# Attention, gated MLP and routed experts on one core: second rows ahead of weights, later conversions, sink work moved to other engines and queues, three fillers

## Chip, cores and metric

The kernel runs on 1 core of one Trainium2 chip. The metric is the device time of one launch in microseconds (us), inputs and outputs in HBM; lower is better.

## What is computed

Three layers, one after the other, all in float32 from outside:

```
scores = q @ k.T / sqrt(64)            # 2 batches, 8 heads, 768 tokens, head size 64
keep   = (key < 4) | (0 <= query - key < 128)      # 4 sink columns and a window
x = softmax(where(keep, scores, -1e9)) @ v         # heads side by side: 1536 x 512
x = (silu(x @ w_gate) * (x @ w_val)) @ w_out       # 512 -> 1536 -> 512
skip = x @ w_skip > 0                              # rows that are computed
e, g = argmax, softmax probability of x @ w_gate2  # one of 8 experts
out  = x + g * (relu(x @ w1[e]) @ w2[e])           # else out = x
```

The three weights of the middle layer come as 64-bit numbers and are turned into float32 on the chip.

## The kernel before

**Staging.** The 1536 tokens are 12 blocks of 128 (block n; six blocks to a batch), in three groups of four. The attention of the first group runs alone; this stretch is called the prologue here. Then the first phase of the MLP starts: TensorE works through the gate, value and down projections of the first group, and the attention of the next blocks and the conversion of the later weights are played between its matmuls from a written score (`beside_first_phase`, `first_phase`). Two more MLP phases, the routing and the experts follow.

**One block of attention.** A block has four head pairs; step j is pair `pr` of block `n`, j = 4n + pr. `step_a` turns k and q of a pair on TensorE (`tqk`, L315) and copies them from PSUM to the tile `kq` (L320); for the first block of a batch GpSimd copies the four sink columns (L331). `step_b` makes the scores (`s`, L363), merges two key blocks by a predicated copy (L369), adds the mask and takes the maximum on VectorE (L380), and takes the exponential on ScalarE (L385), two instructions for a pair. Then it copies the four sink columns of the two heads to `psk` (L399). `step_d` turns the probabilities (`tpt`, L412), copies them out (`pt`) and cuts them by two selections on GpSimd (L422, L423). `step_s` splits the sink columns of a block into a high and a low part (`ps`, L430 and the helper L81) and turns them (`tsk`, L434); `step_e` adds all products with the values (`xps`, L452, L469), divides by the sums (`rps`, L460, L476) and writes the turned block `xt`, high and low, which the MLP reads. `load_sinks` (L277) brings the values of the sink tokens to the tile `vst` and spreads them to `vs` (L291).

**Weights.** `load_w` loads one chunk of 128 columns (or rows) of a weight, 512 KB as 64-bit numbers, to one of three staging buffers `st` (L160). `convert` makes float32 of it: two ScalarE instructions (L175, L176), then two VectorE instructions (L181, L182); then the next chunk is loaded. Chunks come as gate, value, out. `filler` puts matmuls on an idle tile at a very low priority, to be placed where TensorE would wait (L619), `warm` nineteen of them at the start (L608).

**What sets the order.** In the prologue the framework's scheduler orders the instructions of each engine by priorities that follow the order in the code, under the dependencies; each engine then executes its list strictly in order, and a wait of its first instruction holds all that are behind it. An `issue_after` ties an instruction behind another. The first four conversions are tied behind instructions that are noted in `begun`. DMAs of SyncE (SP) and ScalarE are issued in the order of those lists. The loop that drives it all (from L1507) advances attention by one piece per turn (a "pull"), adds fillers, and converts a weight whenever `converted < 12 * pulls // 56`. From the first phase on the order is written by hand and is the same in both kernels, apart from a few fillers at its start.

## Time and profile before

| what | value |
|---|---|
| median of 3 runs | 599.38 us (597.09 to 600.08) |
| profiled execution, its own time | 596.77 us |
| its span (first to last instruction) | 594.4 us |
| TensorE busy | 562.4 us (95%) |
| VectorE, ScalarE, GpSimd busy | 447.1 (75%), 355.1 (60%), 216.5 us (36%) |
| first matmul of the MLP starts at | 63.67 us |
| mean granted TensorE clock | 0.987 |

Times in the rows below count from the start of the span. The profiled execution's own time is 2.37 us longer than its span (launch and end), and lies 2.6 us below the median of the runs. A busy share is an average over stages with different limits, and a TensorE that is shown busy may be waiting inside a pipelined matmul. In a row of the timeline the number behind the start is the duration, and the bracket says how long the engine had been idle and who released it.

### The profile page before, as it was taken

To read this page: it belongs to the slowest core of one execution; us is meant where nothing else is said; L and a number is where in the kernel's file an instruction comes from. 1 tells how busy PE (TensorE), PEld (TensorE's weight loads), DVE (VectorE), ACT (ScalarE), POOL (GpSimd) and SP (SyncE) were. 2 spreads that over 40 slices of the span, in tenths; PEclk is the share of its full clock that TensorE was granted. 3 is DMA by queue.
4 is the path that set the end of the run, shared out by engine and by line. 5 is a ranking of instruction groups with operands and counts; after the bars stand their busy time and mean duration, and the time that the engine had idled before them with its cause. 6 is when DMAs were issued, how large, how long until landed. Compare 5 with 4: busy or idle time off the path is not lost. (4 is left out here: it accounts for less than half of the span.)

```text
span 594.4 us, 10013 instructions
## 1 busy us (share of the span) xinstructions
PE 562.4 (95%) x3052; PEld 437.3 (74%) x3052; DVE 447.1 (75%) x1104; ACT 355.1 (60%) x854; POOL 216.5 (36%) x325
## 2 busy tenths in 40 slices
PE   7999899998999999999999999999998899889992
PEld 4666677786778777787778888888885687667872
DVE  4898587878887899965555999775375797989930
ACT  4798687876776665555454453545164775856710
POOL 3354274676486242413320100040144334525301
PEclk8799999999999999999999999999999999999998
DMA  8896254695523413000004432320268876868501
GB/s 202 196 247 168 83 161 141 178 291 150 162 33 97 139 28 81 1 19 1 18 9 145 149 103 66 99 81 21 84 218 245 276 254 218 313 219 295 187 4 38
DMA packets 90341, 80.53 MB, mean 135 GB/s; under 512 B 53515, under 2 KB 65803, under 8 KB 90274
## 3 DMA queue, kind: packets, MB, share of 16 engines
q1 hardware_dynamic: 87138, 73.01, 41.4%
q0 software_dynamic: 2848, 6.74, 3.7%
q8 instruction: 29, 0.48, 0.3%
q14 instruction: 38, 0.31, 0.2%
q10 hardware_dynamic: 288, 0.00, 0.0%
HBM read 70.09 MB, written 12.00 MB: 138 GB/s over the span
## 5 line engine op out<-in xcount | busy, mean ns | idle before, releaser
L660 PE MATMUL gv<-xt,ring 128*128 128x512 f32 x864 | 218.1, 400 | 1.7 <-ACT xt L78 1.5
L660 PEld LDWEIGHTS gv<-xt,ring 128*128 128x128 f32 x864 | 158.3, 188 | 40.7 <-issue 2.5
L78 ACT ACTIVATE ring<-w 128x512 fp32r<-128x512 f32 x113 | 70.8, 628 | 71.1 <-PE gv L660 54.8
L81 DVE TENSOR_TENSOR w<-stage,w 128x512 fp32r<-128x512 f32 x99 | 87.6, 924 | 4.8 <-ACT w L78 3.4
L78 ACT ACTIVATE w<-stage 128x512 fp32r<-128x512 f32 x128 | 74.2, 627 | 19.8 <-DMA stage<-in_moe_w_dram 15.6
L673 PE MATMUL acc<-ring,hh 128*128 128x512 f32 x256 | 82.4, 403 | 0.0
L81 DVE TENSOR_TENSOR ring<-w,ring 128x512 fp32r<-128x512 f32 x77 | 53.8, 699 | 25.3 <-ACT ring L78 21.6
L81 POOL TENSOR_TENSOR w<-stage,w 128x512 fp32r<-128x512 f32 x29 | 39.9, 1380 | 88.5 <-DVE ring L81 60.1
L81 POOL TENSOR_TENSOR ring<-w,ring 128x512 fp32r<-128x512 f32 x36 | 48.8, 1362 | 32.1 <-ACT ring L78 30.3
L673 PEld LDWEIGHTS acc<-ring,hh 128*128 128x128 f32 x256 | 46.3, 188 | 11.7 <-issue 1.0
L869 DVE CUSTOM_DVE_ANT_0 wl<-x,wl 128x512 f32<-128x512 f32 x72 | 51.5, 716 | 1.3
L673 PE MATMUL acc<-ring,hl 128*128 128x512 f32 x128 | 50.6, 396 | 0.0
L1226 PE MATMUL yps<-w,hT 128*128 128x512 f32 x192 | 48.3, 401 | 0.8 <-ACTq L1265 0.4
L422 POOL TENSOR_SCALAR_AFFINE_SELECT pt<-pt 128x256 f32<-128x256 f32 x40 | 23.6, 591 | 67.7 <-ACT pt L78 67.7
L385 ACT ACTIVATE p<-p,st 128x132 f32<-128x132 f32 x96 | 38.1, 399 | 15.9 <-DVE st L380 13.9
L1226 PEld LDWEIGHTS yps<-w,hT 128*128 128x128 f32 x192 | 35.1, 188 | 10.7 <-DVE hT L81 1.3
L1197 PE MATMUL hps<-w,xh 128*128 128x512 f32 x128 | 41.5, 405 | 1.2 <-PEq L1265 0.3
L181 DVE SCALAR_TENSOR_TENSOR st<-st 128x512 int32<-128x512 int32 x36 | 31.1, 864 | 4.7 <-ACT st L175 4.7
L363 PE MATMUL s<-kq 64*128 64x260 f32 (+1 forms) x144 | 30.8, 416 | 2.9 <-DVE st L380 1.8
L182 DVE SCALAR_TENSOR_TENSOR w<-w,st 128x512 int32<-128x512 int32 x36 | 32.0, 890 | 1.9
L78 ACT ACTIVATE hh<-th 128x512 fp32r<-128x512 f32 (+1 forms) x36 | 21.0, 583 | 18.2 <-DVE th L744 13.2
L924 POOL DMA_INDIRECT xs<-x,pi x12 | 12.3, 1025 | 53.2 <-DVE pi L913 50.1
(203 smaller groups left out, 947.9 us busy)
## 6 DMA issues: line engine op xcount, KB each, us to landing
stage<-in_moe_w_dram SPq DMA_DIRECT2D x128, 256.0 KB
st<-in_moe_w_gate_dram SPq DMA_DIRECT2D x12, 512.0 KB
st<-in_moe_w_val_dram SPq DMA_DIRECT2D x12, 512.0 KB
st<-in_moe_w_out_dram SPq DMA_DIRECT2D x12, 512.0 KB
xs<-trash SPq DMA_DIRECT2D x8, 387.0 KB
vb<-in_v_dram SPq DMA_DIRECT2D x12, 256.0 KB
out_dram<-x SPq DMA_DIRECT2D x12, 256.0 KB
wl<-wgt SPq DMA_DIRECT2D x10, 256.0 KB
```

Of the source, the lines that this page charges most:

```text
L78: nc.scalar.activation(out=out, in_=in_, func=ACTF.Copy, scale=scale, bias=bias)
L81: return (eng or nc.vector).tensor_tensor(out=out, in0=in_, in1=hi.bitcast(F32), op=ALU.subtract).ins
L181: nc.vector.scalar_tensor_tensor(out=low, in0=high, scalar=-0x80000000, in1=low, op0=ALU.bitwise_and, op1=ALU.bitwise_or)
L182: nc.vector.scalar_tensor_tensor(out=di, in0=di, scalar=3, in1=low, op0=ALU.logical_shift_left, op1=ALU.bitwise_or)
L363: m_ = nc.tensor.matmul(out=ss[h][:, 0:nk], lhsT=x_, rhs=y_, start=m == 0, stop=m == len(terms) - 1)
L385: nc.scalar.activation(out=p[:, h], in_=p[:, h], func=ACTF.Exp, scale=-1.0, bias=st[:, h:h + 1], accum_out=su[:, h:h + 1])
L422: nc.gpsimd.affine_select(out=d[:, 0], in_=d[:, 1], compare_op=ALU.is_ge, fill=0.0, base=0, pattern=[[0, 2], [1, P]], channel_multiplier=-1)
L660: nc.tensor.matmul(out=ps, lhsT=w_[:, kk * P:(kk + 1) * P], rhs=x_[:, kk, t0 * P:t1 * P], start=kk == 0 and m == 0, stop=kk == KD - 1 and ...
L673: nc.tensor.matmul(out=acc[g, t], lhsT=h_[:, s], rhs=w_, start=c == 0 and m == 0, stop=c == last and m == 2)
L869: nc.vector.tensor_tensor_reduce(out=junk, in0=x2s[t][:, 0:DM], in1=row, scale=1.0, scalar=0.0, op0=ALU.mult, op1=ALU.add, accum_out=lp[:, ...
L1197: nc.tensor.matmul(out=ps[half], lhsT=x_[:, kk, :], rhs=w_[:, kk, :], start=kk == 0 and m == 0, stop=kk == KD - 1 and m == 2)
L1226: nc.tensor.matmul(out=y, lhsT=h_[:, c, :], rhs=w_[:, c % 4, :], start=c == 0 and m == 0, stop=c == NF2 - 1 and m == 2)
```

## The change

It touches the prologue alone. (1) The k and q rows of block 1 are loaded ahead of the first three weight chunks instead of between them. (2) The first four conversions are tied behind the exponential of pair 1 instead of behind its `kq` copy. (3) The sink values of the first batch are loaded at the very start from ScalarE's queue; their split is tied behind the first masked scores. (4) The copies to `psk` and the split to `ps` of the first four blocks go from VectorE to GpSimd. (5) The `kq` copies of pairs 1 and 3 of blocks 1 to 3 go from ScalarE to VectorE, six in all. (6) In the first 17 pulls three fillers are put in instead of one.

```diff
--- before.py
+++ after.py
@@ -277,7 +277,7 @@
     def load_sinks(b):
         st = sm.tile([96, D], F32, tag="vst", name="vst", bufs=1)
         for a in range(3):
-            nc.sync.dma_start(out=st[32 * a:32 * a + 32], in_=v[b, :, 0:4, :])
+            (nc.sync if b else nc.scalar).dma_start(out=st[32 * a:32 * a + 32], in_=v[b, :, 0:4, :])
         yield
         hi = sm.tile([96, D], F32R, tag="vsh", name="vsh", bufs=1)
         lo = sm.tile([96, D], F32, tag="vsl", name="vsl", bufs=1)
@@ -317,9 +317,11 @@
         o = (i % 2) * W
         src = t[:, 0:2 * P].rearrange("p (a f) -> p a f", a=2)
         if whole(n):
-            c_ = nc.scalar.activation(out=two(kq[0, pr], o, KW - o), in_=src, func=ACTF.Copy)
-            if j == 1:
-                begun["ACT"] = c_.ins
+            dst = two(kq[0, pr], o, KW - o)
+            if i and n < GS and pr % 2:
+                nc.vector.tensor_copy(dst, src)
+            else:
+                act_copy(dst, src)
         else:
             hi, lo = (two(kq[hl, pr], o, KW - o) for hl in range(2))
             act_copy(hi, src)
@@ -382,7 +384,9 @@
             begun.setdefault("DVE", r_.ins)
         yield
         for h in range(2):
-            nc.scalar.activation(out=p[:, h], in_=p[:, h], func=ACTF.Exp, scale=-1.0, bias=st[:, h:h + 1], accum_out=su[:, h:h + 1])
+            c_ = nc.scalar.activation(out=p[:, h], in_=p[:, h], func=ACTF.Exp, scale=-1.0, bias=st[:, h:h + 1], accum_out=su[:, h:h + 1])
+        if j == 1:
+            begun["ACT"] = c_.ins
         prob[j] = p
         if n >= LATE_SUM:
             act_copy(su, su, bias=1e-9)
@@ -396,7 +400,7 @@
             invert(sums[n])
         if pr == 0:
             psk[n] = sm.tile([P, H, 4], F32, tag="psk", name="psk")
-        (nc.vector if n < GS else nc.gpsimd).tensor_copy(psk[n][:, 2 * pr:2 * pr + 2], p[:, :, (1 - odd) * P:(1 - odd) * P + 4])
+        nc.gpsimd.tensor_copy(psk[n][:, 2 * pr:2 * pr + 2], p[:, :, (1 - odd) * P:(1 - odd) * P + 4])
 
     def step_d(j):
 
@@ -425,10 +429,9 @@
     def step_s(n):
         src = psk.pop(n)
         ps = sm.tile([P, 3, H, 4], F32R, tag="ps", name="ps", bufs=1)
-        e_ = nc.vector if n < GS else nc.gpsimd
         for a in range(2):
-            e_.tensor_copy(ps[:, a], src)
-        lo_of(ps[:, 2], src, ps[:, 0], e_)
+            nc.gpsimd.tensor_copy(ps[:, a], src)
+        lo_of(ps[:, 2], src, ps[:, 0], nc.gpsimd)
         yield
         t = (acqp if n < GS else attp).tile([P, 512], F32, tag="acq" if n < GS else "att", name="tsk")
         nc.tensor.transpose(out=t[0:96, 0:P], in_=ps.bitcast(F32).rearrange("p a h j -> p (a h j)"), identity=ident)
@@ -484,6 +487,8 @@
     def attention():
 
         done = 0
+        sinks = load_sinks(0)
+        next(sinks)
         warm(19)
         run(step_a(0))
         run(step_a(1))
@@ -502,7 +507,8 @@
                 with tc.issue_after(begun["DVE"]), tc.issue_after(begun["POOL"]):
                     rest()
             if j == 1:
-                run(load_sinks(0))
+                with tc.issue_after(begun["DVE"]):
+                    run(sinks)
             run(step_b(j + 1))
             yield done
             if pr == 0 and n > 0:
@@ -1488,10 +1494,9 @@
     load_first_qk()
     load_v(0)
     make_consts()
-    load_w()
-    load_w()
     run(load_qk(1))
-    load_w()
+    for _ in range(3):
+        load_w()
     at = attention()
     done = 0
     pulls = 0
@@ -1507,7 +1512,7 @@
     while done < GS:
         done = next(at)
         pulls += 1
-        filler(1)
+        filler(3 if pulls < 18 else 1)
         if pulls == 20:
             load_gates()
         while converted[0] < 12 * pulls // 56:
```

The scheduler makes new lists of it. On ScalarE, around the first conversion (`st`, `w32`), the list of before, from the first `kq` copy on; `p` are the exponentials:

```order
L320 ACTIVATE kq00_179<-tqk_180 128x2x128
L320 ACTIVATE kq01_185<-tqk_186 128x2x128
L175 ACTIVATE st_150<-st_150 128x512
L176 ACTIVATE w32_96<-st_150 128x4x128
L385 ACTIVATE p_212,sums_214<-p_212,st_213 128x132 x2
L320 ACTIVATE kq02_223<-tqk_224 128x2x128
L385 ACTIVATE p_246,sums_214<-p_246,st_247 128x132 x2
L78 ACTIVATE pt_257<-tpt_254 128x256
L320 ACTIVATE kq03_260<-tqk_261 128x2x128
L78 ACTIVATE pt_300<-tpt_297 128x256
L320 ACTIVATE kq00_179<-tqk_308 128x256
L175 ACTIVATE st_152<-st_152 128x512
```

and of the changed kernel (its `kq` copies go through the helper L78):

```order
L78 ACTIVATE kq00_183<-tqk_184 128x2x128
L78 ACTIVATE kq01_189<-tqk_190 128x2x128
L78 ACTIVATE kq02_229<-tqk_230 128x2x128
L387 ACTIVATE p_216,sums_218<-p_216,st_217 128x132 x2
L387 ACTIVATE p_254,sums_218<-p_254,st_255 128x132
L78 ACTIVATE kq03_272<-tqk_273 128x2x128
L387 ACTIVATE p_254,sums_218<-p_254,st_255 128x132
L78 ACTIVATE pt_267<-tpt_264 128x256
L175 ACTIVATE st_153<-st_153 128x512
L176 ACTIVATE w32_96<-st_153 128x4x128
L387 ACTIVATE p_299,sums_218<-p_299,st_300 128x132 x2
L78 ACTIVATE pt_312<-tpt_309 128x256
```

The first conversion stood ahead of all exponentials and now stands behind those of pairs 0 and 1, two more `kq` copies and one `pt`.

On TensorE at the same place, before (`tqk_308` are the rows of block 1, the two of them apart; fillers left out):

```order
L412 MATMUL tpt_254<-ident_108,p_212 128x128 x2
...
L315 MATMUL tqk_308<-ident_108,qk_154 128x128
L363 MATMUL s0_285<-kq02_223 128x132
L363 MATMUL s1_286<-kq02_223 128x132
L412 MATMUL tpt_297<-ident_108,p_246 128x128 x2
L315 MATMUL tqk_308<-ident_108,qk_154 128x128
```

and after (`tqk_322` are the rows of block 1):

```order
L315 MATMUL tqk_322<-ident_108,qk_150 128x128 x2
L416 MATMUL tpt_264<-ident_108,p_216 128x128
...
L365 MATMUL s0_295<-kq02_229 128x132
L416 MATMUL tpt_264<-ident_108,p_216 128x128
...
L416 MATMUL tpt_309<-ident_108,p_254 128x128
L365 MATMUL s1_296<-kq02_229 128x132
L315 MATMUL tqk_359<-ident_108,qk_150 128x128 x2
```

The transposes of block 1's rows now stand ahead of the first turned probabilities and of the scores of pair 2, so these wait for the transfer of those rows too.

On GpSimd at the end of the prologue, after (`pt_934` belongs to the last pair; before, no `psk` or `ps` of the first four blocks stood there, only the selections):

```order
L426 AFFINE_SELECT pt_896<-pt_896 128x256
L427 AFFINE_SELECT pt_896<-pt_896 128x256
L403 COPY psk_745<-p_883 128x8
L433 CAST ps_939<-psk_745 128x32 x2
L81 TENSOR_TENSOR ps_939<-psk_745,ps_939 128x32
L426 AFFINE_SELECT pt_934<-pt_934 128x256
L427 AFFINE_SELECT pt_934<-pt_934 128x256
```

The sink columns of the last block are split between the selections of the last two pairs.

## Rows read from the trace of the kernel before

**Rows 1.** Engines by stage: busy us (instructions), granted clock, DMA share, GB/s.

```profile
core 0: us, PE busy (x) PEld busy (x) DVE busy (x) ACT busy (x) POOL busy (x), PEclk, DMA share, GB/s
...
0.00:63.67 63.67, 55.58 (x408) 37.42 (x408) 45.13 (x193) 46.46 (x144) 26.24 (x52) 0.92 0.76 197
63.67:420.00 356.33, 354.22 (x1849) 278.27 (x1850) 279.64 (x712) 216.33 (x532) 128.51 (x212) 1.00 0.33 94
```

**Rows 2.** Timeline of ScalarE, 6 to 10 us: start, duration, operation, idle before it.

```profile
6.18 0.66 ACT L320 ACTIVATE kq<-tqk 128x256 f32<-128x256 f32 x2 [3.12 <-PE tqk L315]
9.29 0.68 ACT L175 ACTIVATE st<-st 128x512 int32<-128x512 uint16 x1 [2.46 <-DMA st<-in_moe_w_gate_dram]
```

**Rows 3.** Timeline of VectorE, TensorE and SyncE's queue at the start.

```profile
8.17 0.08 DVE L380 DVE_READ_ACCUMULATOR2_ANT st<- 128x1 f32 x1
...
10.67 2.31 SPq L280 DMA_DIRECT2D vst<-in_v_dram  x3
...
12.19 0.45 PE L315 MATMUL tqk<-ident,qk 128*128 128x128 f32 x1 [0.29 <-DMA qk<-in_k_dram]
...
15.04 0.19 DVE L284 CAST vsh<-vst 96x64 fp32r<-96x64 f32 x1 [1.90 <-DMA vst<-in_v_dram]
```

**Rows 4.** Timeline of ScalarE, 24 to 31 us, where it hardly waits.

```profile
24.68 0.40 ACT L385 ACTIVATE p<-p,st 128x132 f32<-128x132 f32 x1
...
25.07 0.37 ACT L320 ACTIVATE kq<-tqk 128x256 f32<-128x256 f32 x1
25.33 0.40 ACT L385 ACTIVATE p<-p,st 128x132 f32<-128x132 f32 x1
...
28.14 0.71 ACT L175 ACTIVATE st<-st 128x512 int32<-128x512 uint16 x1
...
29.28 0.40 ACT L320 ACTIVATE kq<-tqk 128x256 f32<-128x256 f32 x1
...
30.89 0.68 ACT L176 ACTIVATE w<-st 128x512 f32<-128x512 f32 x1
```

**Rows 5.** Engines by stretch of the prologue, columns as in rows 1.

```profile
0.00:9.29 9.29, 6.84 (x36) 4.48 (x37) 3.79 (x27) 1.94 (x3) 2.62 (x17) 1.00 0.70 177
9.29:20.00 10.71, 8.89 (x37) 5.50 (x37) 7.13 (x27) 7.80 (x27) 5.56 (x7) 0.62 1.03 241
24.00:50.00 26.00, 24.12 (x195) 16.34 (x193) 23.32 (x90) 25.19 (x79) 13.04 (x18) 1.00 0.81 218
```

**Rows 6.** Groups of instructions, VectorE in the prologue: count, busy us, mean ns.

```profile
L182 DVE SCALAR_TENSOR_TENSOR w<-w,st 128x512 int32<-128x512 int32 x12 | 9.0, 746 | 0.3
...
L399 DVE COPY psk<-p 128x8 f32<-128x8 f32 x16 | 4.3, 270 | 3.4 <-ACT p L385 3.3
...
L430 DVE CAST ps<-psk 128x32 fp32r<-128x32 f32 x8 | 1.3, 205 | 0.0
...
L81 DVE TENSOR_TENSOR ps<-psk,ps 128x32 fp32r<-128x32 f32 x4 | 0.9, 234 | 0.0
```

**Rows 7.** Groups of instructions over the whole span, VectorE and GpSimd.

```profile
L399 POOL COPY psk<-p 128x8 f32<-128x8 f32 x32 | 11.3, 352 | 24.8 <-ACT p L78 12.0 <-DVE p L391 8.1 <-ACT th L740 2.9
L430 POOL CAST ps<-psk 128x32 fp32r<-128x32 f32 x16 | 4.3, 301 | 0.5
L81 POOL TENSOR_TENSOR ps<-psk,ps 128x32 fp32r<-128x32 f32 x8 | 3.8, 480 | 0.0
...
L859 DVE COPY x2T<-x2t 128x256 f32<-128x256 f32 x1 | 0.4, 424 | 0.3 <-PE x2t L853 0.3
```

**Rows 8.** Timeline of TensorE: fillers at either clock level.

```profile
14.00 0.85 PE L619 MATMUL warm<-ident 128*128 128x256 bf16 x3
...
27.38 0.60 PE L619 MATMUL warm<-ident 128*128 128x256 bf16 x4
```

**Rows 9.** Timeline at 18 us: a GpSimd and a VectorE instruction side by side.

```profile
18.27 1.03 POOL L291 TENSOR_TENSOR vs<-vsh,bm 32x512 fp32r<-32x512 f32 x1
...
18.49 1.36 DVE L182 SCALAR_TENSOR_TENSOR w<-w,st 128x512 int32<-128x512 int32 x1
```

## Prediction

> **What bounds the kernel now.** I read the stages first [rows 1]. From the first matmul of the MLP at 63.67 us to 420 us TensorE is busy for 354.2 of 356.3 us at the full clock: this part cannot be shortened by what is moved in the prologue, it only starts earlier or later, and all behind it with it. In the prologue the number to see is different: TensorE 55.6 of 63.7 us, but fillers are among that, and the two engines that make something are VectorE (45.1) and ScalarE (46.5). So the question is when the first matmul of the MLP starts, and I follow the engine that paces the prologue.
>
> That is ScalarE: between 24 and 50 us it is busy for 25.2 of 26 us, VectorE for 23.3 [rows 5]. Ahead of 24 us it is not: the waits show why. At 9.29 us the first conversion starts after 2.46 us of waiting for the first weight chunk [rows 2], while VectorE had finished the maximum for the first exponential at 8.17 + 0.08 = 8.25 us [rows 3]; ScalarE executes in order, so the exponentials stood behind the weights. At 12.19 us TensorE waits for the k rows of block 1, and at 15.04 us VectorE has waited 1.90 us for the sink values, whose loads were only issued at 10.67 us [rows 3]; the masked scores of pair 2 stand behind that wait.
>
> **The change, part by part.** I walk along ScalarE's new list to an instruction that both lists have, the second half of the sixth conversion (L176), which starts at 30.89 us before [rows 4].
>
> The prices are distances from start to start, not durations, since neighbours overlap there [rows 4]: an exponential 25.07 - 24.68 = 0.39 us; a copy of 128x256 25.33 - 25.07 = 0.26; a conversion with both halves 29.28 - 28.14 = 1.14, so half of it, or another pass of 512 columns, 0.57.
>
> *Start of the walk: the first weight chunk.* It landed at 9.29 us, when 9.29 x 177 GB/s = 1.64 MB had moved [rows 5]. Now the k and q rows of block 1, two tiles of 128x8x64 numbers or 0.52 MB, go ahead of it; at the 241 GB/s of the next stretch [rows 5] that is 2.2 us, so 11.5 us. What stands ahead of the first conversion on ScalarE is hidden in front of that: four exponentials, two `kq` and one `pt` copy, 4 x 0.39 + 3 x 0.26 = 2.3 us from 8.25, so done by 10.6. The rows of block 1, for which the first turned probabilities now wait on TensorE, have as many bytes up to their end (block 0's q, k, v and their own: 1.3 MB) as the first weight chunk had before, and should land near 9.3; if they come late, `pt` and the rest are late by as much, which is the second rival.
>
> *From there to the sixth conversion:* five conversions, 5.70; half a one, 0.57; ten exponentials, 3.90; nine copies of 256 columns or fewer (five `pt`, three `kq`, one for the turned sink columns), 2.34; two passes of 512 (the inverse sums and `xt`), 1.14. Sum 13.65 us, so L176 starts at 25.15 us without any wait: 5.7 us earlier. The same sum for the kernel before, with four more exponentials and six more copies, is 13.65 + 1.56 + 1.56 = 16.8 of the 21.6 us from 9.29 to 30.89; so 4.8 us were waits. Between 0 and 4.8 us of waits is the bound for the new list too. I take 1.0: the second out chunk, for the sixth conversion, has 5.5 MB up to its end; 1.64 MB at 9.29 us and 241 GB/s after it give 25.3 us, and the walk is there at 23.8. Weights alone may flow faster, so I take two thirds of the 1.5. **Gain up to here 4.7 us.**
>
> *Later in the prologue,* where ScalarE has no gaps, three of the six `kq` copies that leave it are still to come (the first three are in the walk): 3 x 0.26 = 0.8 us. On VectorE the six cost 0.42 us each, by the one copy of that shape from PSUM that the trace has [rows 7]: 2.5 us in. What leaves VectorE is 4.3 + 1.3 + 0.9 = 6.5 us [rows 6], so it is 4.0 us lighter and doesn't take over as pacer. **Gain 5.5.**
>
> *Sink work on GpSimd:* 16 x 0.352 + 8 x 0.301 + 4 x 0.480 = 9.9 us [rows 7], on an engine that is busy for 26.2 of 63.7 us [rows 1]. It is beside other work except at the end, where the last block's copy, two casts and subtraction are a link of the chain to `xt`: 1.43 us there, against 0.27 + 0.33 + 0.23 = 0.83 on VectorE [rows 6, 7]; between 0 and 0.6 us, I take 0.3.
>
> *Fillers:* 34 more, of which 28 stand ahead of the first MLP matmul. Four take 0.60 us at the full clock, three 0.85 at half of it [rows 8]; all in the way would be 28 x 0.15 = 4.2 us or more, but they are placed where TensorE is expected to wait. Bounds: 0 to 4.2 us of loss; I take 0.3. In return they may hold the clock, which was granted at 0.62 on average from 9.29 to 20 us [rows 5] (1.2 GHz in most of it) after 1.00, 2.4 GHz, up to then; I count nothing for that, since TensorE doesn't pace there.
>
> *Sink loads on ScalarE's queue:* three issues took 2.31 us on SP [rows 3]; ScalarE is idle for 3.12 us ahead of its first copy [rows 2], so they are hidden. If that cover were gone, the first copy would be late by what exceeds it.
>
> Sum: 5.7 - 1.0 + 0.8 - 0.3 - 0.3 = **4.9 us less**. The profiled execution would go from 596.77 to 591.9 us, the first MLP matmul from 63.67 to 58.8. The runs' median is 599.38, 2.6 above that execution; I give the time against the median: **594.5 us**. About 0.5%, or 3.0 us, is what a measurement of this kernel tells from no change: 596.4 to 602.4.
>
> **The rivals.** *1. More is gained* (8%): no wait at all in the walk and a shorter end of the prologue, since it has slack that I left as it is: 7.5 us, 591.9. For it speaks that VectorE gets lighter; against it that the last steps are one chain.
>
> *2. Transfers pace the first rows* (18%). The DMA share is already 1.03 from 9.29 to 20 us [rows 5], and the change asks for the same bytes some 5 us earlier. If the first chunk comes at 13.5 instead of 11.5 and the sixth conversion waits another 0.9 us, 2.9 of the 4.9 us are lost: 597.4. Against it: the share over the whole prologue is only 0.76 [rows 1].
>
> *3. GpSimd holds VectorE up, and the change is slower* (17%). Beside GpSimd's spreading of the sink values (1.03 us) a second conversion step on VectorE took 1.36 us [rows 9] instead of 0.75 [rows 6]. The place is the stretch from 10 us on: 28 instructions more on GpSimd. VectorE has 26 - 23.3 = 2.7 us of slack there [rows 5] and 4.0 us of relief; once the 24 conversion steps on it are lengthened by more than that 6.7, VectorE paces, and once by 6.7 + 4.9 = 11.6 us, or 0.48 us each (a mean of 1.23 us instead of 0.75), the gain is gone. With all of them at 1.36 they take 14.6 us more, and the loss of 7.9 leaves +3.0: 602.4. Against it: GpSimd's own new pieces are short. The Trainium skill, page "SBUF — State Buffer", section "Who interferes with whom", says that the two engines share one pair of SBUF ports, and that a GpSimd instruction that reads SBUF and a VectorE instruction with two SBUF inputs fully block one another. The trace agrees with that in rows 9. By that rule, with each of GpSimd's new instructions blocking VectorE for its whole time, VectorE would get 9.9 - 4.0 = 5.9 us more, 3.2 beyond its slack, and the time would be 597.7. Of the 17 I give 8 to a lengthening that takes part of the gain and 9 to one that takes it all.
>
> *The change does not do what it says* in one point at most: the clock may stay at half. As nothing is counted for it, the sum stands.
>
> **How the numbers follow.** Forecast 57%: its bounds are no wait and no loss (6.5 us, 592.9) and some 3 us of gain (596.4); 55 of these count as faster, 2 as the same. With rival 1 all faster (8), rival 2 with 4 faster, 13 same, 1 slower, rival 3 with 8 same, 9 slower: faster 0.67, same 0.23, slower 0.10. The range leaves out the slower half of rival 3 and the utmost of rival 1: 590.5 to 600.5.
>
> **What would show it.** Right: the first exponential starts near 8.3 us; the first conversion near 11.5, behind four exponentials; no wait of VectorE for the sink values; the sixth conversion's L176 near 26 us; the first MLP matmul near 59 us, and the span after that matmul unchanged within 1 us. Wrong: ScalarE waiting for weight DMAs by more than 2 us after the first (rival 2); VectorE's conversion steps with a mean over 1 us (rival 3); TensorE waiting for the rows of block 1 beyond 11 us; or a gain in the prologue that is lost after 64 us, in which case the step that fails is that the rest only moves.

## Result and the profile after

The changed kernel is slower: 602.15 us in the median of 20 runs against 599.73 for the kernel before, ratio 1.0082 (95% interval 1.0055 to 1.0108). The ratio, like all below, leaves out runs in a slower state with a lower granted clock; the medians of all runs differ by 0.4%. The profiled execution has a span of 598.0 us (before 594.4), and the first matmul of the MLP starts at 67.20 us instead of 63.67: 3.5 of the 3.6 us between these two executions are lost in the prologue.

Stages and stretches of the changed kernel (columns as in [rows 1]):

```profile
core 0: us, PE busy (x) PEld busy (x) DVE busy (x) ACT busy (x) POOL busy (x), PEclk, DMA share, GB/s
0.00:67.20 67.20, 58.88 (x436) 40.45 (x437) 44.63 (x171) 45.38 (x138) 30.44 (x80) 0.92 0.72 187
67.20:423.53 356.33, 354.56 (x1853) 278.43 (x1852) 278.73 (x712) 216.51 (x532) 129.32 (x212) 1.00 0.33 94
...
24.00:50.00 26.00, 22.14 (x173) 15.18 (x169) 22.02 (x69) 21.15 (x63) 15.42 (x32) 0.93 0.75 213
45.00:50.00 5.00, 5.00 (x25) 3.19 (x25) 3.12 (x17) 3.70 (x14) 2.18 (x9) 0.66 0.52 152
...
11.75:29.90 18.15, 17.66 (x113) 11.84 (x114) 12.42 (x45) 14.13 (x44) 6.45 (x16) 0.82 0.90 221
```

The MLP behind the prologue did not change: the 356.33 us from its first matmul on are filled as in [rows 1]. From 24 to 50 us ScalarE is busy for 21.15 instead of 25.19 us [rows 5], and it no longer paces. The last row is the stretch of the walk, from the first conversion to L176 of the sixth: TensorE is busy for 17.66 of 18.15 us, ScalarE for 14.13.

The first steps, ScalarE's timeline after the change (compare [rows 2, 4]):

```profile
8.13 0.41 ACT L387 ACTIVATE p<-p,st 128x132 f32<-128x132 f32 x1 [0.29 <-DVE st L382]
...
11.75 0.67 ACT L175 ACTIVATE st<-st 128x512 int32<-128x512 uint16 x1
...
12.88 0.39 ACT L387 ACTIVATE p<-p,st 128x132 f32<-128x132 f32 x1
...
18.18 0.38 ACT L78 ACTIVATE pt<-tpt 128x256 f32<-128x256 f32 x1 [2.05 <-PE tpt L416]
18.46 0.66 ACT L175 ACTIVATE st<-st 128x512 int32<-128x512 uint16 x1
...
29.90 0.68 ACT L176 ACTIVATE w<-st 128x512 f32<-128x512 f32 x1
```

Down to 12.88 us every step of attention is earlier, and the first conversion later, as meant; then ScalarE waits 2.05 us for a turned probability. TensorE's timeline shows why (L625 are fillers, `tpt` the turned probabilities, `s` the scores), and VectorE what hangs on it:

```profile
15.19 0.82 PE L625 MATMUL warm<-ident 128*128 128x256 bf16 x3
15.80 0.63 PE L315 MATMUL tqk<-ident,qk 128*128 128x128 f32 x2
16.23 0.84 PE L625 MATMUL warm<-ident 128*128 128x256 bf16 x3
16.87 0.42 PE L416 MATMUL tpt<-ident,p 128*128 128x128 f32 x1
17.08 0.84 PE L625 MATMUL warm<-ident 128*128 128x256 bf16 x3
17.72 0.42 PE L416 MATMUL tpt<-ident,p 128*128 128x128 f32 x1
17.94 0.69 PE L625 MATMUL warm<-ident 128*128 128x256 bf16 x3
18.55 0.71 PE L365 MATMUL s<-kq 64*128 64x260 f32 x4
...
19.29 0.30 DVE L371 COPY_PREDICATED s<-above,s 128x128 f32<-128x128 int32 x1 [2.72 <-PE s L365]
```

Twelve fillers, most of them at half clock, stand among two turned probabilities and the next scores: 2.5 us from start to start, of the 3.36 us from 15.19 to 18.55. TensorE takes its list in order.

The second place is the second block. GpSimd (L81 `ring` subtracts a weight piece; L403, L433 and L81 `ps` are the sink columns), VectorE, TensorE and ScalarE:

```profile
32.30 1.27 POOL L81 TENSOR_TENSOR ring<-w,ring 128x512 fp32r<-128x512 f32 x1
33.51 0.19 POOL L403 COPY psk<-p 128x8 f32<-128x8 f32 x1
33.76 0.36 POOL L433 CAST ps<-psk 128x32 fp32r<-128x32 f32 x2
34.08 0.25 POOL L81 TENSOR_TENSOR ps<-psk,ps 128x32 fp32r<-128x32 f32 x1
...
36.96 1.29 POOL L81 TENSOR_TENSOR ring<-w,ring 128x512 fp32r<-128x512 f32 x1 [0.35 <-ACT ring L78]
...
39.88 1.46 POOL L81 TENSOR_TENSOR ring<-w,ring 128x512 fp32r<-128x512 f32 x1 [1.03 <-ACT ring L78]
...
37.05 1.74 DVE L181 SCALAR_TENSOR_TENSOR st<-st 128x512 int32<-128x512 int32 x1
...
40.30 1.58 DVE L182 SCALAR_TENSOR_TENSOR w<-w,st 128x512 int32<-128x512 int32 x1
41.81 0.68 DVE L479 TENSOR_TENSOR rs<-xps,rs 128x512 f32<-128x512 f32 x1
...
34.39 0.31 PE L437 MATMUL tsk<-ident,ps 128*96 128x128 f32 x1 [1.38 <-POOL ps L81]
...
43.84 0.67 PE L365 MATMUL s<-kq 64*128 64x260 f32 x2 [2.32 <-DVE st L382]
...
42.52 0.63 ACT L78 ACTIVATE xt<-rs 128x512 fp32r<-128x512 f32 x1 [1.32 <-DVE rs L479]
```

A weight subtraction was ordered ahead of the sink columns, and TensorE waits 1.38 us for them. Two more come beside VectorE's conversion steps, which take 1.74 and 1.58 us instead of about 0.7. The kernel before has the same three subtractions on GpSimd, but they start behind the division of the second block (39.62 us): two in this row, the third at 53.42:

```profile
39.93 3.01 POOL L81 TENSOR_TENSOR ring<-w,ring 128x512 fp32r<-128x512 f32 x2
```

In the changed kernel the division L479, all that hangs on it, and the scores at 43.84 are late, TensorE stands idle for 2.32 us, and right after that its granted clock is 0.66 from 45 to 50 us. The division of block 0 came at 25.34 us (before 25.94), that of block 1 at 41.81 (39.62): the gain was 0.6 us and the loss 2.2 one block later.

### The profile page after: what moved, and what is told of

It reads as the page before. It is cut to its first block, busy times and chain, and to the rows that moved or that the text cites. A ratio compares the mean times of both kernels' runs of the same rounds, so it can differ in the third digit from the quotient of the medians.

```text
span 598.0 us, 10066 instructions
## 1 busy us (share of the span) xinstructions
PE 567.3 (95%) x3086; PEld 442.0 (74%) x3086; DVE 444.8 (74%) x1082; ACT 353.6 (59%) x848; POOL 222.0 (37%) x353
## 5 line engine op out<-in xcount | busy, mean ns | idle before, releaser
L78 ACT ACTIVATE ring<-w 128x512 fp32r<-128x512 f32 x113 | 71.1, 629 | 71.0 <-PE gv L666 54.7
L81 DVE TENSOR_TENSOR w<-stage,w 128x512 fp32r<-128x512 f32 x99 | 87.0, 918 | 6.8 <-ACT w L78 5.6
L78 ACT ACTIVATE w<-stage 128x512 fp32r<-128x512 f32 x128 | 73.6, 627 | 21.2 <-DMA stage<-in_moe_w_dram 16.8
L81 POOL TENSOR_TENSOR w<-stage,w 128x512 fp32r<-128x512 f32 x29 | 40.5, 1398 | 90.8 <-DVE ring L81 60.1
L81 DVE TENSOR_TENSOR ring<-w,ring 128x512 fp32r<-128x512 f32 x77 | 54.1, 703 | 25.2 <-ACT ring L78 22.3
L81 POOL TENSOR_TENSOR ring<-w,ring 128x512 fp32r<-128x512 f32 x36 | 49.5, 1380 | 32.1 <-ACT ring L78 30.3
L426 POOL TENSOR_SCALAR_AFFINE_SELECT pt<-pt 128x256 f32<-128x256 f32 x40 | 22.0, 551 | 55.5 <-ACT pt L78 55.5
L365 PE MATMUL s<-kq 64*128 64x260 f32 (+1 forms) x144 | 32.3, 414 | 4.7 <-DVE st L382 3.0
L371 DVE COPY_PREDICATED s<-above,s 128x128 f32<-128x128 int32 x80 | 20.4, 288 | 16.2 <-PE s L365 16.1
L182 DVE SCALAR_TENSOR_TENSOR w<-w,st 128x512 int32<-128x512 int32 x36 | 30.8, 854 | 2.0
```

Of the source, the lines that this page charges most:

```text
L78: nc.scalar.activation(out=out, in_=in_, func=ACTF.Copy, scale=scale, bias=bias)
L81: return (eng or nc.vector).tensor_tensor(out=out, in0=in_, in1=hi.bitcast(F32), op=ALU.subtract).ins
L182: nc.vector.scalar_tensor_tensor(out=di, in0=di, scalar=3, in1=low, op0=ALU.logical_shift_left, op1=ALU.bitwise_or)
L365: m_ = nc.tensor.matmul(out=ss[h][:, 0:nk], lhsT=x_, rhs=y_, start=m == 0, stop=m == len(terms) - 1)
L426: nc.gpsimd.affine_select(out=d[:, 0], in_=d[:, 1], compare_op=ALU.is_ge, fill=0.0, base=0, pattern=[[0, 2], [1, P]], channel_multiplier=-1)
```

## Experiments

Ratios are to the kernel before, with their 95% intervals. "First MLP matmul" is from the one profiled execution of each version; as will be seen, it moves by 2.6 us from one execution of a version to another, so the ratio decides.

**One filler.** The changed kernel without part 6:

```diff
-        filler(3 if pulls < 18 else 1)
+        filler(1)
```

> The changed kernel with one filler a pull again (part 6 undone, the rest kept). Theory A, fillers: four groups of three fillers at half clock stand in TensorE's list from 15.2 to 18.6 us ahead of the turned probabilities and scores of pairs 2 and 3 and cost 2 to 3 us. Then the scores after 18.55 us come by 16.5, L176 of the sixth conversion starts by 28 us (29.90 with three fillers), the first MLP matmul near 64.5 us (67.20), ratio to the kernel before about 1.003. Theory B, sink work on GpSimd: L176 moves by less than 0.7 us, the first MLP matmul stays near 66.7, ratio about 1.007.

0.9929 (0.9888 to 0.997): 1.5% less than with three. The profiled execution, though, had the clock at half from 11 to 31 us, L176 of the sixth conversion at 34.39 us (theory A: by 28) and its first MLP matmul at 66.9 us (64.5); of the 4.2 us by which its span is shorter than the changed kernel's, only 0.3 lie ahead of that matmul. Theory A has the sign of the ratio, which moved by more than it asked for (1.003), but its signs in the trace missed.

**Sink columns on VectorE.** The changed kernel without part 4:

```diff
-        nc.gpsimd.tensor_copy(psk[n][:, 2 * pr:2 * pr + 2], p[:, :, (1 - odd) * P:(1 - odd) * P + 4])
+        (nc.vector if n < GS else nc.gpsimd).tensor_copy(psk[n][:, 2 * pr:2 * pr + 2], p[:, :, (1 - odd) * P:(1 - odd) * P + 4])
+        e_ = nc.vector if n < GS else nc.gpsimd
-            nc.gpsimd.tensor_copy(ps[:, a], src)
-        lo_of(ps[:, 2], src, ps[:, 0], nc.gpsimd)
+            e_.tensor_copy(ps[:, a], src)
+        lo_of(ps[:, 2], src, ps[:, 0], e_)
```

> The changed kernel with the sink columns of the first four blocks on VectorE again (part 4 undone), three fillers kept. Theory B: TensorE's waits for GpSimd's split sink columns (1.38 us at 34.4, 0.64 at 61.4) and part of VectorE's long steps beside GpSimd go: first MLP matmul near 64.5 us instead of 67.20, ratio to the kernel before about 1.003; L176 of the sixth conversion, which is ahead of all this, stays near 29.9. Theory A: the first MLP matmul stays within 1 us of 67.2, ratio 1.006 to 1.009. Theory C, the copies of k and q on VectorE and the reordered list are at fault: as for A.

1.0022 (0.9984 to 1.0061), first MLP matmul at 63.2 us, no wait for GpSimd. So part 4 also carries a part of the loss, as B had it (though L176 of the sixth conversion moved to 32.24 us and did not stay near 29.9): either edit undone alone takes most of it back, and the two don't simply add.

**Both undone.** The last two diffs together; parts 1, 2, 3 and 5 are left.

> Parts 4 and 6 both undone: the early rows, the tie of the conversions, the sink loads and the six copies of k and q on VectorE are left. Theories A and B together (each some 2.5 us, and the gain of the first steps is real): first MLP matmul at 60 to 62 us, ratio to the kernel before 0.994 to 0.997. Theory C: it stays above 63.5 us, ratio 1.000 or more.

0.996 (0.9923 to 0.9998). A gain of the size that A and B together asked for, but not better than with the sink columns on GpSimd (0.9929): with one filler part 4 costs nothing that these ratios show. The first MLP matmul was at 65.9 us, where A and B together had 60 to 62; that execution, with 602.14 us, is among the longer of its version.

**Parts 1 to 3 alone.** As the last, and:

```diff
-            if i and n < GS and pr % 2:
-                nc.vector.tensor_copy(dst, src)
-            else:
-                act_copy(dst, src)
+            act_copy(dst, src)
```

> Parts 1 to 3 alone (rows of block 1 ahead of the weights, first conversions behind the exponential of pair 1, sink values from ScalarE's queue); parts 4 to 6 undone. The forecast's walk gives 4.7 us less the three copies of k and q in it (0.8), so 3.9: first MLP matmul near 59.8 us, ratio 0.9935. Theory C: faster than the run with the six copies on VectorE by 1 us or more. If transfers pace the first rows after all (rival 2), it is within 1 us of the kernel before, 62.7 to 64.7 us, with ScalarE waiting over 2 us for weight DMAs after the first conversion.

0.9997 (0.9958 to 1.0037), first MLP matmul at 62.6 us. The forecast's main term, 3.9 us of gain by these parts, is missing, and no weight DMA is waited for (rival 2 falls). ScalarE's waits from 9.5 to 25 us:

```profile
ACT pt L78 <- PE tpt L413: 3.2, 3, 1.7
ACT p L384 <- DVE st L379: 1.2, 2, 0.6
ACT skT L78 <- PE tsk L435: 1.2, 1, 1.2
```

It waits mostly for TensorE, which from 10.3 to 27.7 us never waits itself.

**Fillers alone, sink columns on GpSimd alone.** Part 6, and part 4, each put into the kernel before:

```diff
-        filler(1)
+        filler(3 if pulls < 18 else 1)
```

```diff
-        (nc.vector if n < GS else nc.gpsimd).tensor_copy(psk[n][:, 2 * pr:2 * pr + 2], p[:, :, (1 - odd) * P:(1 - odd) * P + 4])
+        nc.gpsimd.tensor_copy(psk[n][:, 2 * pr:2 * pr + 2], p[:, :, (1 - odd) * P:(1 - odd) * P + 4])
-        e_ = nc.vector if n < GS else nc.gpsimd
+        e_ = nc.gpsimd
```

> The kernel before with part 6 alone (three fillers instead of one in the first 17 pulls). Theory A, fillers cost by themselves what the changed kernel with and without them differ by (1.0082 against 0.9929, 9 us): ratio to the kernel before 1.008 to 1.015, and the 28 additional fillers stand in front of turned probabilities and scores that were ready. Theory D, they cost only where the early rows have made the first steps come faster than TensorE can go: in the kernel before, whose ScalarE stood behind the weights at 9.29 us, they fall into idle time, ratio 0.998 to 1.003.

> The kernel before with part 4 alone (sink columns of the first four blocks on GpSimd). Theory B: GpSimd's split stands ahead of TensorE's transposition of the sink columns in each of the four blocks, and VectorE's long steps beside it: ratio 1.004 or more. By the pair of runs with one filler (0.9929 with part 4, 0.996 without it) it costs nothing: ratio 0.995 to 1.002, as VectorE's relief of 6.5 us makes good what the link costs.

Part 6: 1.0024 (0.9981 to 1.0066), no difference that can be measured, as theory D said: by themselves the fillers are not what the changed kernel loses. Its profiled execution even had the first MLP matmul at 61.2 us, with half clock from 9 to 15.5 us (before 63.67, and 12 to 22); the ratio shows no gain from that. Part 4: 1.0087 (1.0033 to 1.014), a loss of its own, as B said and against the guess from the pair with one filler. TensorE's longest group of waits there, and two of VectorE's conversion steps beside weight subtractions on GpSimd:

```profile
PE tsk L434 <- POOL ps L81: 3.0, 4, 1.0
...
41.64 1.69 DVE L181 SCALAR_TENSOR_TENSOR st<-st 128x512 int32<-128x512 int32 x1
51.89 1.77 DVE L182 SCALAR_TENSOR_TENSOR w<-w,st 128x512 int32<-128x512 int32 x1
```

**Two repeats,** without an edit, of the changed kernel and of its version with one filler:

> The changed kernel unaltered, on the same chip as its version with one filler, for a second profile. Theory A: ratio 1.006 to 1.011 again; first MLP matmul within 1 us of 67.2, the four groups of three fillers at half clock from 15 to 19 us in the same place. If the first MLP matmul moves by more than 2 us from one execution to the next, single profiles do not rank the versions and only the medians do.

> The changed kernel with one filler a pull, again, for a second profile: in the first the clock was at half for some 20 us from 11 to 31 us and the first MLP matmul at 66.9 us, which a ratio of 0.9929 does not fit. Theory A: ratio 0.990 to 0.997 again; in an execution with the clock back at full by 24 us, as in the kernel before, the first MLP matmul comes at 60 to 63 us. If the clock stays at half beyond 28 us here too, the gain of this version must lie behind the first MLP matmul.

1.0045 (1.0001 to 1.0089) and 0.9944 (0.9899 to 0.9989). The changed kernel repeats itself in detail: first MLP matmul at 67.3 us, half clock from 11 to 17.5 and from 45 to 48.5 us (first 11.5 to 18 and 45.5 to 49). The version with one filler doesn't: half clock from 9 to 19 and 43 to 46.5, first MLP matmul at 64.2 us instead of 66.9. Single profiles don't rank these versions. In this second profile, although the subtractions stand behind the sink columns, two of VectorE's steps ahead of the second block's division (39.57 us) take 1.61 and 0.95 us, TensorE is then idle for 1.21 us, and half clock follows: one filler has the same trouble in a milder form.

**Three fillers early, or late.** The changed kernel with

```diff
-        filler(3 if pulls < 18 else 1)
+        filler(3 if pulls < 9 else 1)
```

and with `3 if 9 <= pulls < 18 else 1`:

> The changed kernel with three fillers only in pulls 1 to 8 (the first steps, where the clock is at half) and one from pull 9 on. Over the runs so far the time goes with the mean granted clock by 584 us per unit, that is 0.49 us for each us at half clock; at equal clock three fillers in all 17 pulls cost 5 us beside the early rows and 0.9 us in the kernel before. Theory A1, the early ones cost (they stand at half clock ahead of turned probabilities): ratio 1.003 to 1.008, the scores of pair 4 at 18.5 us as in the changed kernel. Theory A2, the later ones cost (26 fillers in 3.3 us of full clock at 26 to 31 us): ratio 0.992 to 0.998, half clock for some 6.5 us at the start as with three everywhere, first MLP matmul 63 to 64.5 us.

> The changed kernel with three fillers only in pulls 9 to 17 and one before. Theory A1: ratio 0.992 to 0.998, as with one filler everywhere, scores of pair 4 by 17.5 us. Theory A2: ratio 1.003 to 1.008. If the cost is in both, this and the run with the early ones are both near 1.000.

1.0096 (1.0032 to 1.016) and 1.016 (1.009 to 1.023): both theories miss. Halving the fillers made it no better in either half, so their own time is not the larger part of the loss. What all three versions with part 4 and more than one filler share is GpSimd's list: a weight subtraction ahead of the second block's sink columns (from 33.14 and 32.11 us here), with a wait of TensorE of 1.3 and 1.4 us for them; with one filler it stands behind them. The version with the late ones shows what happens when the clock goes (columns as above):

```profile
48.00:54.00 6.00, 6.00 (x17) 2.81 (x16) 2.30 (x10) 2.92 (x9) 1.49 (x6) 0.50 0.52 149
```

From 48 to 54 us TensorE is busy all the time at half clock, and VectorE for 2.30 and ScalarE for 2.92 of 6 us: they wait for it. First MLP matmul at 73.1 us.

**No fillers.** Parts 1 to 3 alone, with

```diff
-        filler(1)
+        filler(0 if pulls < 18 else 1)
```

> Parts 1 to 3 alone, with no filler in the first 17 pulls. Theory E, TensorE paces the first steps while its clock is at half (with one filler it never waits from 10.9 to 28 us, and ScalarE and VectorE wait for it): without the 11 fillers of 10.4 to 20 us, 0.21 us each, the scores of pair 4 (17.65 us with one filler) come by 16 us. If the clock stays at half longer for want of fillers, the first MLP matmul comes later than the 62.6 us of the version with one filler by 1 to 4 us, ratio 1.000 to 1.006; if not, 61 us and 0.995. If ScalarE paces, as the forecast had it, nothing moves by more than 0.5 us.

0.9882 (0.9822 to 0.9942) from 6 runs, first MLP matmul at 60.2 us. Theory E holds. TensorE up to the scores of step 4 (the first of block 1), with one filler and then with none:

```profile
15.62 1.25 PE L623 MATMUL warm<-ident 128*128 128x256 bf16 x5
16.66 0.63 PE L413 MATMUL tpt<-ident,p 128*128 128x128 f32 x2
17.09 0.64 PE L623 MATMUL warm<-ident 128*128 128x256 bf16 x2
17.65 1.24 PE L362 MATMUL s<-kq 64*128 64x260 f32 x4
```

```profile
14.69 0.69 PE L413 MATMUL tpt<-ident,p 128*128 128x128 f32 x2
15.31 1.24 PE L362 MATMUL s<-kq 64*128 64x260 f32 x4
```

2.34 us earlier, the time of the 11 fillers; and the clock was back at full at 18.5 us, not later than with them (21.5). ScalarE has the same 52 instructions in both versions from the first conversion to L176 of the sixth (columns as above, one filler and then none):

```profile
12.30:32.07 19.77, 18.84 (x112) 12.29 (x112) 14.07 (x58) 15.85 (x52) 4.25 (x6) 0.76 0.89 216
```

```profile
12.42:29.49 17.07, 15.50 (x96) 9.73 (x96) 15.25 (x60) 15.69 (x52) 5.40 (x7) 0.82 1.02 246
```

Its waits there fall from 3.9 to 1.4 us.

**A bridge.** Parts 1, 2, 3 and 5 with one filler, and four of the same matmuls tied directly behind the scores of pair 0 and of pair 1:

```diff
         run(step_b(0))
+        bridge(4)
         yield 0
...
             run(step_b(j + 1))
+            if j == 0:
+                bridge(4)
```

> Parts 1, 2, 3 and 5 with one filler a pull, and four more matmuls of the same kind behind the scores of pair 0 and of pair 1, in the first steps' idle time of TensorE (7 to 10 us). Theory E: if they hold the clock at full beyond 9 to 11.5 us, or shorten the stretch at half clock from 10 us to 5, TensorE's list of the first block is done 2 to 4 us earlier: first MLP matmul at 59 to 61 us, ratio 0.988 to 0.993. If the clock falls all the same for as long, ratio 0.995 to 1.000 and the eight fillers cost up to 1 us. If the clock doesn't matter there, it is held and the time stays at 0.996.

0.996 (0.9916 to 1.0004), as without the bridge, and first MLP matmul at 63.4 us. The clock was held, but only put off:

```profile
12.00:20.00 8.00, 7.76 (x55) 5.17 (x56) 6.88 (x36) 7.39 (x24) 1.49 (x4) 1.00 1.01 240
...
27.50:34.50 7.00, 6.92 (x29) 4.13 (x31) 5.38 (x27) 5.32 (x19) 2.46 (x6) 0.51 0.45 140
```

At full clock ScalarE is busy for 7.39 of 8 us from 12 to 20: there it paces, as the forecast had it. Behind TensorE's waits of 0.65, 0.89 and 0.87 us from 23 to 28 us the clock fell for some 6.5 us, and the lead was given back.

**The kernel before without fillers, and two more without.** `filler(0 if pulls < 18 else 1)` in the kernel before, in the version with parts 1, 2, 3 and 5, and in the changed kernel:

> The kernel before with no filler in the first 17 pulls. If the gain of 1.2% that parts 1 to 3 had without fillers is the fillers' alone, this gives 0.985 to 0.991 too. Theory E: in the kernel before the early fillers fall mostly into TensorE's waits behind the first conversion and the late k rows, so less is gained: 0.993 to 0.999, first MLP matmul 61.5 to 63.5 us. If the clock stays at half longer for want of them: 1.000 to 1.005.

> Parts 1, 2, 3 and 5 with no filler in the first 17 pulls. With one filler part 5 went from 0.9997 to 0.996, so if that is part 5's own gain: 0.983 to 0.987 (without part 5 0.9882), first MLP matmul 58.5 to 60 us. If VectorE's copies stand in front of its maxima once TensorE is no longer late: 0.989 to 0.993.

> The changed kernel without any filler in the first 17 pulls: parts 1 to 5. Theory B (part 4 costs 0.5 to 1% by itself): 0.990 to 0.996, slower than the same without part 4 by 3 to 6 us, with TensorE waiting 1 to 2 us for GpSimd's split sink columns. If part 4 costs only where a weight subtraction comes ahead of the sink columns (here it comes behind those of the second block): within 1.5 us of the version without part 4.

1.0039 (0.9998 to 1.008), 0.9992 (0.995 to 1.0035) and 0.996 (0.9929 to 0.9991). In the kernel before it gains nothing in time: the gain of the no-filler version needs the early rows, or the clock that it had. First MLP matmuls are at 63.7, 63.8 and 65.2 us, the first two later than expected, behind half clock from 10 to 23.5, 12 to 29 and 11 to 31.5 us. Part 5, which seemed to help with one filler, costs about 1% without any, and part 4 costs nothing there, as its second branch had it. Why part 5 costs is open; it goes with the clock, whose mean over its runs was 0.974, against 0.982 without it.

**The weight subtractions moved.** The changed kernel with

```diff
-        lo_of(lv, s, hv, nc.gpsimd if nm in LO[ph] else nc.vector)
+        lo_of(lv, s, hv, nc.gpsimd if nm in LO[ph] and (ph or c) else nc.vector)
```

> The changed kernel with the subtractions of the first prepared weight pieces on VectorE instead of GpSimd, three fillers kept; so no weight subtraction stands on GpSimd ahead of the second block's sink columns, and VectorE's conversion steps beside them (1.74 and 1.58 us in the changed kernel) are not held up. Theory F, that GpSimd's list is the larger part of the loss: no clock fall at 45 us, first MLP matmul at 62.5 to 64.5 us instead of 67.2, ratio 0.997 to 1.002. Theory A, that it is the fillers: the scores of pair 4 stay at 18.5 us, first MLP matmul within 1.5 us of 67.2, ratio 1.005 to 1.010.

0.9984 (0.9949 to 1.002), first MLP matmul at 64.2 us: theory F. All 34 additional fillers and the sink work on GpSimd are still there; the loss is not. GpSimd, VectorE and TensorE at the same place:

```profile
33.84 0.19 POOL L403 COPY psk<-p 128x8 f32<-128x8 f32 x1
34.10 0.36 POOL L433 CAST ps<-psk 128x32 fp32r<-128x32 f32 x2
34.42 0.25 POOL L81 TENSOR_TENSOR ps<-psk,ps 128x32 fp32r<-128x32 f32 x1
...
37.99 0.68 DVE L81 TENSOR_TENSOR ring<-w,ring 128x512 fp32r<-128x512 f32 x1
38.59 0.68 DVE L182 SCALAR_TENSOR_TENSOR w<-w,st 128x512 int32<-128x512 int32 x1
...
34.72 0.31 PE L437 MATMUL tsk<-ident,ps 128*96 128x128 f32 x1 [0.34 <-DVE st L382]
...
41.88 0.67 PE L365 MATMUL s<-kq 64*128 64x260 f32 x2 [0.23 <-DVE st L382]
```

TensorE's wait for the sink columns is 0.34 instead of 1.38 us, the conversion step takes 0.68, the scores of 43.84 come at 41.88, and the clock stays at full from 24 to 50 us. The edit takes away both the subtraction ahead of the sink columns and those beside the conversion steps ahead of the division, so it doesn't tell which of the two counted.

**Last two.** The no-filler version again, and the last edit with one filler:

> Parts 1 to 3 alone with no filler in the first 17 pulls, again. At equal clock (time corrected by the slope over all runs) the three versions with early rows and no filler agree within 0.8 us, some 4.5 us below the kernel before; the raw ratios differ by the mean clock (0.982 here the first time, 0.974 in the others). If that was chance: ratio 0.994 to 0.999 now, mean clock near 0.975. If this order holds the clock better: 0.986 to 0.992 again, half clock only from 12 to 18.5 us in the profile.

> The changed kernel with one filler a pull and the first weight subtractions on VectorE: both causes undone. If they add up (fillers 5 us and weight subtractions 3 us at equal clock): 0.986 to 0.991. If the fillers cost so much only through the order of the weight subtractions on GpSimd: 0.992 to 0.996, as with one filler alone (0.9929 and 0.9944).

0.9863 (0.9813 to 0.9913) and 0.998 (0.9938 to 1.0022). The no-filler version repeats its ratio, but not its profile: half clock from 9.5 to 20 us and the first MLP matmul at 62.2 us, in an execution of 600.61 us, the longest of its seven. Parts 1 to 3 without fillers beat the kernel before by 1.2 to 1.4%, and by their two ratios the changed kernel by some 2%. The two causes don't add, and 0.998 lies above both forecasts: with one filler the subtractions are behind the sink columns anyway, and moving them gains nothing. With the subtractions moved, three fillers (0.9984) and one (0.998) are the same.

**All runs together.** Each run has a time and a mean clock. Over 362 of the 366 (a line with one slope, and a level for each version) the time falls by 589 us per unit of clock: one us more at half clock, 0.5/598 of the mean, goes with 0.5 us more time. Left out are three runs of 696 us and more, and one run of the kernel before, 601.3 us at a clock of 0.927, which alone would pull the slope to 476. The slope is not a price of the prologue's clock: the two profiled executions of the no-filler version, 591.24 and 600.61 us, differ by 2.0 us ahead of the first MLP matmul and by 7.3 us behind it, where the order of instructions is the same. The levels at a clock of 0.98, in us, and each version's own mean clock:

| version | no filler | one | three |
|---|---|---|---|
| kernel before | 596.0 (0.970) | 598.6 (0.979) | 599.7 (0.980) |
| parts 1 to 3 | 594.3 (0.983) | 597.2 (0.978) | |
| parts 1, 2, 3, 5 | 593.9 (0.974) | 596.1 (0.976) | 600.9 (0.982) |
| parts 1 to 5 | 593.2 (0.974) | 597.1 (0.982) | 602.1 (0.980) |
| parts 1 to 5, subtractions moved | | 598.1 (0.978) | 599.6 (0.984) |

At the same clock fillers always cost: the first 2.6 us in the kernel before, 2.2 to 3.9 with the early rows; the next two 1.1 in the kernel before, 4.8 to 5.0 with the early rows, and 1.5 once the subtractions are moved. What they give back is clock, and not in every row. These are levels of a fit, not measurements of single versions; the ratios above are those.

## Why the prediction was wrong

*The first steps were right.* First exponential 8.13 us (forecast 8.25), first conversion 11.75 (11.5) behind four exponentials and without a wait for DMA, VectorE not waiting for the sink values, rows of block 1 at 10.16 us, within the 11 named. That the MLP behind the prologue only moves is right too.

*The step that failed is "TensorE doesn't pace there".* It took the gain away; the two terms below, fillers and sink work, made a loss of it. The walk goes along ScalarE's list and allows 1.0 us of waits, all for transfers, out of bounds of 0 to 4.8. It measured 18.15 - 14.13 = 4.0 us in the profiled execution, none of it for transfers, and L176 of the sixth conversion came at 29.90 instead of near 26. With the weights out of the way, TensorE, at half clock for some 6.5 us of the stretch, was the next engine, and it was full: 17.66 of 18.15 us. The stretch could have been read beforehand; the kernel before at the same place, from the first conversion to that L176:

```profile
9.29:30.89 21.60, 19.14 (x113) 12.41 (x113) 15.54 (x63) 17.32 (x56) 8.41 (x11) 0.76 0.89 216
```

TensorE has 19.14 us of work there, more than the 13.65 us that the walk has from the first conversion on. The prediction had set this aside because "fillers are among that"; but they stand in the list, in order. The pair of parts 1 to 3 shows it: with one filler ScalarE waits for 3.9 us in the walk and nothing is gained; without fillers it waits for 1.4 (1.6 in the second execution), near the forecast's 1.0, and the ratio gains 1.2 to 1.4%. That list has two more exponentials and four more copies than the changed kernel's; by the forecast's prices it takes 13.65 + 0.78 + 1.04 = 15.47 us without waits, and ScalarE was busy for 15.69. The first MLP matmul came at 60.2 and 62.2 us, where 58.8 was forecast for all six parts.

*The fillers were mis-sized:* 0.3 us of bounds 0 to 4.2. By the fit it is 4.8 to 5.0 us beside the early rows, beyond the upper bound, 1.1 in the kernel before, and 1.5 with the subtractions moved; so in the changed kernel most of it goes through GpSimd's list and not through the fillers' own time. "They are placed where TensorE is expected to wait" was the error: the early rows had removed those waits.

*The sink work on GpSimd was priced by its durations,* at 0.3 us and "beside other work except at the end". Its durations were even shorter than assumed; but it is a link of the chain in every block (alone it cost 0.9%, with four waits of TensorE). What made the changed kernel lose was where GpSimd's weight subtractions came to stand: in all four profiles with sink work on GpSimd, more than one filler and the subtractions there, one is ahead of the second block's sink columns. The run that moved only the subtractions shows that they are the loss: 0.9984 instead of 1.0045 and 1.0082. Whether they cost through the sink columns or through VectorE's steps is not shown.

*Rival 3 had the engines and the sign, not the size or the cause.* VectorE's conversion steps have means of 798 and 764 ns in the prologue, not the 1.23 us at which the rival was to decide, and the two long ones stood beside weight subtractions that both kernels have, not beside the 28 new instructions. They came ahead of the division on which the next block hangs, and TensorE's idle time behind them was followed by 3.5 us of half clock. The Trainium skill, page "SBUF — State Buffer", section "Who interferes with whom", has the two engines exclude each other in such a pair; the steps of 1.74 and 1.58 us beside subtractions of 1.29 and 1.46 agree with it. The price that the prediction worked out by that rule, 597.7 us by one total of blocked time, doesn't say where the blocks fall.

*That the clock may stay at half was given no price.* No run isolates one for the prologue; over all runs 0.5 us goes with each us at half clock, most of it, in the one pair of profiles above, behind the prologue.

What stays open: why part 5 costs 1% once the fillers are gone; by which of its two ways a subtraction on GpSimd costs; where three fillers cost 4.8 us by the fit when no sink work is on GpSimd; and how the changed kernel's loss divides exactly between fillers and order, since the two act on one another.

## What to carry to other kernels

When a wait is taken from the engine that paces, count the work that every other in-order engine has in that same stretch, at the clock granted there, before pricing the gain; fillers and warm-up matmuls count as work as soon as the waits that they were to fill are gone. Work moved to a second engine is priced by what the scheduler puts in front of it there, and not only by its own duration: read the new order of that engine, and look for long instructions ahead of a short one that others wait for. And where the clock moves, rank versions by many runs; a single profile shows the mechanism only.

## What was not expected of the hardware

In the one attempt made, the clock's fall was put off but not avoided: with the bridge TensorE kept 1.00 until 27.5 us, and then had 0.51 for 7 us. In all profiled executions but that one the first spell at half clock began between 8.5 and 12.5 us. It lasted 6.5 to 7 us in both executions of the changed kernel and in the kernel before with three fillers, but some 10 us with three fillers and the weight subtractions moved; with one filler 6.5 to 20 us, and with none 6.5 to 20 as well. One kernel's runs differ by up to 19 us (596.9 to 616.1 with the early fillers), and go with the mean clock (0.981 to 0.959).

The end of the kernel varies too, with the same order of instructions: from the last matmul into `gv` to the end of the span it took 183.2 us in the kernel before (411.2 to 594.4) and 191.2 in the changed kernel without part 4 (410.0 to 601.2), with TensorE waiting up to 3.9 us for one of VectorE's subtractions among the experts. A difference of 5 us between two single executions says nothing there.
